# Attention, gated MLP and soft mixture of experts on one core: matmuls of constants, another order of loads and a moved subtraction in the opening

## The chip, the core and the metric

One core of a Trainium2 chip runs the whole program. It has a matrix engine (TensorE; PE in the profile, its weight loads PEld), three engines for elementwise work (VectorE or DVE, ScalarE or ACT, GpSimd or POOL), a queue engine that issues transfers (SyncE, SP), and 16 DMA engines. Each engine works through its own instructions in program order and waits on semaphores for the others.

The metric is the device time of one execution in microseconds (us). The kernel before takes 543.9 us, the median of three runs that lie between 542.54 and 544.36.

## The reference

Three stages follow one another; the change is in the first, attention with a forgetting gate.

```python
def _attn_ref(q, k, v, f):                      # q, k, v: (4, 8, 576, 64), f: (4, 8, 576)
    scores = scale * np.matmul(q, k.transpose(0, 1, 3, 2))
    cum = np.cumsum(np.log(np.clip(f, 0.0001, 1.0)), axis=-1)
    decay = cum[:, :, :, None] - cum[:, :, None, :]
    scores = np.where(causal, -1000000000.0, scores + decay)
    attn = np.exp(scores - np.max(scores, axis=-1, keepdims=True))
    attn = attn / (np.sum(attn, axis=-1, keepdims=True) + 1e-09)
    return np.matmul(attn, v)

x = attention, laid out as 2304 tokens x 512
h = x @ w_in;  x = (h * sigmoid(h)) @ w_out     # 512 -> 2048 -> 512
return soft_moe(x, phi, w1, w2)                 # 8 experts with 4 slots each, 512 -> 1024 -> 512
```

## The kernel before, in words

The 32 heads are worked off as 16 pairs. A pair's q and k come in one tile (`UB` for pair 0, `qk` after it) of 128 partitions x 2 heads x 576 positions: partitions 0 to 63 hold q, 64 to 127 hold k. The products run in a reduced-precision form of float32, so each operand is split into a high half (a rounded copy, `split_hi`, line 160, on ScalarE) and a low half (what the rounding lost, `split_lo`, lines 166 and 168, a subtraction). `QA` and `KA` hold the high halves of q and k, one over the other in partitions 0 to 63; in partitions 64 and up they hold what adds the decay: two rows of `KA` are the cumulated log gates of a head (`spread`, lines 174 and 176, small transfers), the rows of `QA` that meet them are ones, and row 127 of `QA` later takes the row maxima. `KB` and `QB` hold high and low halves crosswise, so that KA x QA plus KB x QB is the whole score.

Two passes are made over each head. `max_piece` (line 190, tile `mx`, six pieces m0 to m5 a head) multiplies KA with QA alone, and VectorE takes the row maxima (line 196, and 193). Three banks of PSUM turn over for these pieces. `max_fin` transposes the maxima (line 209, tile `mtp`), copies them (line 211) and sends them into row 127 of QA (line 212). `s_piece` (lines 236 and 238, tile `st`, pieces s0 to s4) makes the scores, and ScalarE writes their exponentials to `E` (line 242). GpSimd cuts the diagonal blocks (line 259). `av` (line 293) and `row_sums` (line 277) use E afterwards.

The order of all this is a string, `ORDER`, worked off once for each step i from -6 on, its first half for even i and its second for odd i. In step i the scores of head i and the maxima of head i+3 are made, so the first three heads have their maxima made in steps -3, -2 and -1, without scores beside them, and head 3 in step 0 beside the scores of head 0. The letters q0 to q3 in the first and second half are the four copies of `split_hi`: 0 is QA, 1 KA, 2 the high half in KB, 3 that in QB, in the order q2, q0, q1, q3; for pairs 0 and 1 they come in the steps -4 to -1, two steps a pair. z00 to z11 are the subtractions of `split_lo`. For pair 0 those for k are issued by the main loop itself after step -2, and go to VectorE; all other subtractions go to GpSimd.

Before step -6 `setup` prepares gates, masks and constants: VectorE fills, clips, scans and scales the gates into `cum`, ScalarE takes the logarithm, GpSimd fills the rest. Then the transfers are issued on SP: pair 0 (line 141, two transfers, one a head), the constant rows of QA for pair 1 (line 115, `init_q(1)`), the first head of pair 1, the decays of pairs 0 and 1 (four transfers), the second head of pair 1, the constant rows for pair 2, and pair 2 (line 138). The maxima of a pair need its QA and KA copies, its decays and its constant rows.

After attention come the MLP (`h`, lines 579 to 581) and the mixture of experts, whose code is the same in both kernels.

Of the kernel before, what the change touches and what calls it, by code (L numbers as in the profile page):

```python
# [9 lines left out]
F32 = mybir.dt.float32  # L10
F32R = mybir.dt.float32r
BF16 = mybir.dt.bfloat16
# [19 lines left out]
RING_A, RING_B, RING_T = "014", "235", "b"  # L32
# [3 lines left out]
def tile_attention_moe_softmoe(ctx: ExitStack, tc: tile.TileContext, qk, vr, f, wcat, phi, w1, w2, out):  # L36
# [44 lines left out]

    xs = [xpool.tile([128, 4, CH], F32, name=f"x{c}", tag=f"x{c}", bufs=1) for c in range(NCH)]

    def setup():
        nc.sync.dma_start(out=ft, in_=f)
        nc.vector.memset(c8, 1.0)
        init_k(0)
        init_q(0)
        nc.vector.tensor_scalar(ft, ft, 1e-4, 1.0, ALU.max, ALU.min)
        nc.scalar.activation(ft, ft, AF.Ln)  # L90
        nc.vector.memset(nbias, -float(896 << 23))
        nc.scalar.activation(warm, nbias[0:1], AF.Exp)
        nc.vector.tensor_tensor_scan(c8, c8, ft, 0.0, ALU.mult, ALU.add)
        nc.vector.tensor_scalar(cum[:, 0], c8, -8.0, None, ALU.mult)
        nc.vector.scalar_tensor_tensor(cum[:, 1], c8, -8.0, cum[:, 0], op0=ALU.mult, op1=ALU.subtract)
        nc.gpsimd.memset(mask, 0.0)
        nc.gpsimd.affine_select(out=mask[:, 320:448], in_=mask[:, 320:448], pattern=[[-1, 128]],
                                compare_op=ALU.is_ge, fill=-1e30, base=0, channel_multiplier=1)
        init_k(1)
        nc.gpsimd.memset(ones, 1.0)  # L100
        one = xs[8][:, 0, 0:128]
        nc.gpsimd.memset(one, 1.0)
        nc.gpsimd.affine_select(out=ident, in_=one, pattern=[[-1, 128]], compare_op=ALU.is_equal,
                                fill=0.0, base=0, channel_multiplier=1)
        init_k(2)
        for j in range(3):
            init_e(j)
# [25 lines left out]
    def load(p, hs=(0, 1)):  # L133
        b, hp = divmod(p, NP)
        if p not in staged:
            staged[p] = UB if p == 0 else ld.tile([128, 2, S], F32, name="qk", tag="qk", bufs=3)
        if p > 1:
            nc.sync.dma_start(out=staged[p], in_=qk[b, hp])
            return
        for h in hs:  # L140
            nc.sync.dma_start(out=staged[p][:, h], in_=qk[b, hp, :, h])
# [11 lines left out]
    def split_hi(p, j):  # L153
        q, k = staged[p][0:64], staged[p][64:128]
        qa = QA[p % 3][0:64, :, 64:640]
        if j == 3 and p > 1:
            nc.sync.dma_start(out=QB.of(p)[0:64].bitcast(F32), in_=qa.bitcast(F32))
        else:
            out = (qa, KA[p % 3][0:64], KB.of(p)[64:128], QB.of(p)[0:64])[j]
            nc.scalar.activation(out, (q, k, k, q)[j], AF.Copy)  # L160

    def split_lo(p, which, h):
        src = staged[p][:, h]
        eng = nc.vector if p == 0 and which == 1 else nc.gpsimd
        if which:
            eng.tensor_tensor(KB.of(p)[0:64, h], src[64:128], KB.of(p)[64:128, h], ALU.subtract)  # L166
        else:
            eng.tensor_tensor(QB.of(p)[64:128, h], src[0:64], QA[p % 3][0:64, h, 64:640], ALU.subtract)  # L168
# [12 lines left out]
    def max_piece(i, j):  # L181
        p, h = divmod(i, 2)
        qa, ka = QA[p % 3], KA[p % 3]
        blk = min(j, 4)
        k0, w = [(0, 64), (0, 192), (0, 320), (0, 448), (0, 288), (288, 288)][j]
        if j == 0 and h == 0:
            Mt[p] = att.tile([128, 2, 5], F32, name="Mt", tag="Mt", bufs=2)
            Mx[p] = att.tile([128, 2, 1], F32, name="Mx", tag="Mx", bufs=2)
        t = bank("b", [128, 512], "mx")
        nc.tensor.matmul(t[:, 0:w], lhsT=qa[0:127, h, 128 * blk:128 * blk + 128], rhs=ka[0:127, h, k0:k0 + w],  # L190
                         start=True, stop=True)
        if j == 4:
            nc.vector.tensor_reduce(Mx[p][:, h], t[:, 0:w], axis=AX.X, op=ALU.max)
        else:
            junk = att.tile([128, 448], BF16, name="junk", tag="junk", bufs=2)
            nc.vector.tensor_tensor_reduce(out=junk[:, 0:w], in0=t[:, 0:w], in1=mask[:, 448 - w:448], scale=1.0,  # L196
                                           scalar=Mx[p][:, h] if j == 5 else -3e38, op0=ALU.add, op1=ALU.max,
                                           accum_out=Mt[p][:, h, blk:blk + 1])
        if j == 5:
            MAXED.add(i)  # L200
# [134 lines left out]
    def att_step(i, cv):  # L335
        p, h = divmod(i, 2)
        s = 0 <= i < NH
        pa = p - 1
        a = 0 <= pa < NPAIR
        mi = i + 3  # L340
        mx = 0 <= mi < NH

        def cvt(n, ph):
            if ph == 0:
                conv_b(n)
            elif ph == 1:
                conv_c(n)
            elif ph == 2:
                conv_d(n, 0)
                conv_d(n, 1)  # L350
            elif ph == 3:
                conv_wh(n)
            elif ph == 4:
                conv_d(n, 2)
                conv_d(n, 3)
            elif ph == 6:
                conv_wl(n)
                conv_f(n)

        for op in ORDER.split("|")[h].split():  # L360
            k, j = op[0], op[1:]
            if k == "s" and s:
                s_piece(i, int(j))
            elif k == "m" and mx:
                max_piece(mi, int(j))
            elif k == "v" and a:
                av(pa, int(j))
            elif k == "r" and a and done["r"] <= pa:
                row_sums(done["r"])
                done["r"] += 1  # L370
            elif k == "q" and 0 <= p + 2 < NPAIR:
                split_hi(p + 2, int(j))
            elif k == "z" and j[0] == "1" and (i + 3) // 2 == 0:
                pass
            elif k == "z" and 0 <= (i + 3) // 2 < NPAIR:
                split_lo((i + 3) // 2, int(j[0]), int(j[1]))
            elif k == "f":
                max_fin()
            elif k == "n" and done["n"] < min(done["r"], NPAIR - 1):
                norm_b(done["n"])  # L380
                done["n"] += 1
            elif k == "b" and done["b"] < done["x"] and done["b"] in READY:
                norm_c(done["b"])
                done["b"] += 1
            elif k == "p" and 1 < p + 3 < NPAIR:
                spread(p + 3)
            elif k == "x" and done["x"] < done["n"]:
                norm_x(done["x"])
                done["x"] += 1
            elif k == "c":  # L390
                for n, ph in cv:
                    cvt(n, ph)
            elif k == "e" and p <= 0:
                max_fin()
            elif k == "k":
                cut()
            elif k == "g":
                pump()
            elif k == "w" and 0 <= p + 1 < NPAIR:
                load_v(p + 1)  # L400
            elif k == "l" and 3 <= p + 3 < NPAIR:
                load(p + 3)
# [562 lines left out]
    with tc.manual_schedule():  # L965
# [5 lines left out]
        for i in range(-6, NH + 2):  # L971
            if i == -6:
                load(0)
                init_q(1)
                load(1, (0,))
                spread(0)
                spread(1)
                load(1, (1,))
                init_q(2)
                load(2)  # L980
                nc.sync.dma_start(out=cumd, in_=cum.bitcast(F32))
            if i in (0, 3, 5):
                mo["cap"] += 1
            if i == 0:
                pump()
            if i == NH - 6:
                ld.release()
                mo["r"] = tc.alloc_tile_pool(name="w1p", bufs=1, side="right", reuse_waits="tile")
                FREE.extend((mo["r"], f"r{j}") for j in range(4))
            cv = [(n, i - b) for n, b in enumerate(CONV_AT) if 0 <= i - b < 7]  # L990
            att_step(i, cv)
            if i == -2:
                split_lo(0, 1, 0)
                split_lo(0, 1, 1)
            if i == NH + SEL:
                mo.update(last=LAST)
                pump()
            if i == NH - 1:
                selectors()
                split_x(0)  # L1000
            elif i == NH:
                FREE.append((nrm, "U2"))
                arena_a()
                split_x(1)
# [215 lines left out]
```

## Time and profile before

| | |
|---|---|
| median of three runs | 543.9 us |
| the profiled execution | 545.5 us, its span 543.8 us |
| PE busy | 506.0 us, 93% of the span |
| DVE, ACT, POOL busy | 335.3, 296.8 and 206.9 us |
| start of the first maxima, the first scores, the first `av` | 9.37, 20.58 and 34.83 us |

The span runs from the first to the last instruction; the execution's own time has 1.7 us around it. PE's 93% is a mean: in the first 40th of the span it is 2 tenths, in the second 6, and from the third (27 us) on mostly 9. [...] The column of the granted clock begins with a fixed 1.00 in this trace, so that in the opening the level is read from the spacing of equal matmuls.

### The profile page before, as it was taken

How to read it: one execution, taken by the hardware profiler on the slowest of the kernel's cores; microseconds unless marked ns; L12 is line 12 of the kernel's file. 1: busy time of each engine (PE TensorE's matmuls, PEld its weight loads, DVE VectorE, ACT ScalarE, POOL GpSimd, SP SyncE). 2: the span in 40 equal slices, each digit the busy share in tenths (PEclk: the TensorE clock that was granted, in tenths of full speed). 3: DMA queues.
4: the chain of work that ended last, by engine and by line, in shares of the span. 5: the costliest groups of instructions: out<-in, count | busy, mean ns of one | idle time of the engine just before them, and what ended most of it. 6: DMA issues, size and time to landing. Idle time of an engine off the chain costs nothing.

```text
span 543.8 us, 11207 instructions
## 1 busy us (share of the span) xinstructions
PE 506.0 (93%) x4115; PEld 374.2 (69%) x4115; DVE 335.3 (62%) x892; ACT 296.8 (55%) x585; POOL 206.9 (38%) x226
## 2 busy tenths in 40 slices
PE   2699999999999999899999999999997999999994
PEld 2487878877777777677776777666664676664562
DVE  6657767776889379998888733565653532335013
ACT  6668989898896666467556553323321433332013
POOL 6478788887888403556447400000000000001000
PEclk9999999999999999999999999999998999999998
DMA  5435575466654467402512109789697728677998
GB/s 147 157 94 172 164 223 170 133 193 165 174 160 103 130 234 298 176 39 65 170 36 121 78 2 317 224 212 296 211 321 216 242 92 328 230 292 274 409 384 330
DMA packets 43819, 105.80 MB, mean 195 GB/s; under 512 B 8148, under 2 KB 16628, under 8 KB 43764
## 3 DMA queue, kind: packets, MB, share of 16 engines
q1 hardware_dynamic: 43764, 105.08, 59.3%
q8 instruction: 32, 0.52, 0.4%
q14 instruction: 23, 0.19, 0.1%
HBM read 82.58 MB, written 17.52 MB: 184 GB/s over the span
## 4 chain that ended last, share of the span: by engine, by line
PE 68%; DVE 11%; DMA 8%; ACT 7%; issue 2%; POOL 2%; SPq 1%; DVEq 0%; POOLq 0%; ACTq 0%
PE h L579 9%; PE h L581 8%; PE h L580 8%; PE av L293 6%; PE mx L190 4%; PE st L236 4%; PE rs L277 4%; PE st L238 4%; DMA gr<-far 3%; PE lp L650 3%; PE gtp L623 3%; PE pp L766 3%; PE so L892 3%; PE h L837 3%; DVE wt L482 1%
## 5 line engine op out<-in xcount | busy, mean ns | idle before, releaser
L579 PE MATMUL h<-w,xh 128*128 128x512 f32 x288 | 119.3, 414 | 3.7 <-DVE gt L600 3.7
L581 PE MATMUL h<-w,xh 128*128 128x512 f32 x288 | 114.2, 397 | 0.0
L580 PE MATMUL h<-w,xl 128*128 128x512 f32 x288 | 114.1, 396 | 0.0
L600 DVE SCALAR_TENSOR_TENSOR gt<-gt,h 128x512 f32<-128x512 f32 (+1 forms) x73 | 48.4, 674 | 70.5 <-ACT gt L593 70.5
L593 ACT ACTIVATE gt<-h 128x512 f32<-128x512 f32 (+1 forms) x73 | 42.7, 590 | 86.4 <-PE h L581 76.5
L242 ACT ACTIVATE E<-st 128x256 f32<-128x256 f32 (+4 forms) x160 | 63.6, 431 | 18.2 <-PE st L238 15.1
L196 DVE CUSTOM_DVE_ANT_0 junk<-mx,mask 128x64 bf16<-128x64 f32 (+3 forms) x128 | 50.0, 415 | 36.9 <-PE mx L190 35.5
L579 PEld LDWEIGHTS h<-w,xh 128*128 128x128 f32 x288 | 54.4, 189 | 22.0 <-DVE gt L600 6.1
L812 POOL MEMSET SM<- 128x512 f32 x2 | 1.1, 531 | 177.8 <-ACT gt L593 175.2
L190 PE MATMUL mx<-KA,QA 127*128 127x64 f32 (+2 forms) x192 | 53.4, 352 | 15.0 <-ACT KA L160 11.6
L581 PEld LDWEIGHTS h<-w,xh 128*128 128x128 f32 x288 | 54.5, 189 | 12.9
L580 PEld LDWEIGHTS h<-w,xl 128*128 128x128 f32 x288 | 54.5, 189 | 11.0
L236 PE MATMUL st<-QA,KA 128*128 128x256 f32 (+2 forms) x192 | 57.6, 310 | 3.9 <-DMA QA<-mr 1.5
L259 POOL TENSOR_SCALAR_AFFINE_SELECT E<-E 128x256 f32<-128x256 f32 (+1 forms) x96 | 42.9, 461 | 31.4 <-ACT E L242 30.3
L238 PE MATMUL st<-QB,KB 128*128 128x256 f32 (+2 forms) x192 | 53.5, 303 | 0.0
L293 PE MATMUL av<-E,VF 128*64 128x320 f32 (+4 forms) x448 | 50.8, 364 | 0.0
L190 PEld LDWEIGHTS mx<-KA,QA 127*128 127x128 f32 x192 | 35.9, 209 | 20.6 <-issue 9.3
L166 POOL TENSOR_TENSOR KB<-qk,KB 64x576 fp32r<-64x576 f32 x30 | 42.4, 1433 | 4.1 <-ACT KB L160 3.1
L168 POOL TENSOR_TENSOR QB<-qk,QA 64x576 fp32r<-64x576 f32 x30 | 42.8, 1428 | 2.5
L236 PEld LDWEIGHTS st<-QA,KA 128*128 128x128 f32 x192 | 36.2, 188 | 8.2 <-ACT E L242 7.3
L293 PEld LDWEIGHTS av<-E,VF 128*64 128x64 f32 x448 | 29.5, 136 | 17.8 <-POOL E L259 0.3
L510 POOL TENSOR_TENSOR raw<-raw 128x512 f32<-128x512 f32 x16 | 25.4, 1590 | 38.8 <-ACT raw L499 31.8
(152 smaller groups left out, 830.7 us busy)
## 6 DMA issues: line engine op xcount, KB each, us to landing
unit<-in_w_dram SPq DMA_DIRECT2D x64, 512.0 KB
raw<-in_w_dram SPq DMA_DIRECT2D x32, 512.0 KB
far<-gb SPq DMA_DIRECT2D x16, 512.0 KB
gr<-far SPq DMA_DIRECT2D x64, 128.0 KB
qk<-in_qk_dram SPq DMA_DIRECT2D x14, 576.0 KB
VF<-in_v_dram SPq DMA_DIRECT2D x16, 320.0 KB
RB<-R SPq DMA_DIRECT2D x32, 144.0 KB
out_dram<-ob SPq DMA_DIRECT2D x18, 256.0 KB
```

Of the source, the lines that this page charges most:

```text
L168: eng.tensor_tensor(QB.of(p)[64:128, h], src[0:64], QA[p % 3][0:64, h, 64:640], ALU.subtract)
L190: nc.tensor.matmul(t[:, 0:w], lhsT=qa[0:127, h, 128 * blk:128 * blk + 128], rhs=ka[0:127, h, k0:k0 + w], start=True, stop=True)
L196: nc.vector.tensor_tensor_reduce(out=junk[:, 0:w], in0=t[:, 0:w], in1=mask[:, 448 - w:448], scale=1.0, scalar=Mx[p][:, h] if j == 5 else - ...
L236: nc.tensor.matmul(t[0:m, o:o + n], lhsT=ka[:, h, k0:k0 + m], rhs=qa[:, h, 64 + q0:64 + q1], start=True, stop=False)
L238: nc.tensor.matmul(t[0:m, o:o + n], lhsT=kb_[:, h, k0:k0 + m], rhs=qb[:, h, q0:q1], start=False, stop=True)
L242: nc.scalar.activation(e[0:m], t[0:m, 0:o], AF.Exp, scale=0.125)
L259: nc.gpsimd.affine_select(out=e, in_=e, pattern=pattern, compare_op=ALU.is_ge, fill=0.0, base=0, channel_multiplier=-1)
L293: nc.tensor.matmul(AVP[p][x][64 * h:64 * h + 64, o0:o0 + n], lhsT=VF[p % 2][:, kb, h], rhs=E[2 * p + h][kb][:, c:c + n], start=kb == 0, st ...
L579: nc.tensor.matmul(o, lhsT=xh[:, d, tok], rhs=w[:, 0], start=(d == 0), stop=False)
L580: nc.tensor.matmul(o, lhsT=xl[:, d, tok], rhs=w[:, 0], start=False, stop=False)
L581: nc.tensor.matmul(o, lhsT=xh[:, d, tok], rhs=w[:, 1], start=False, stop=(d == 3))
L600: nc.vector.scalar_tensor_tensor(g, g, 1.0, h[:, n * j:n * j + n], op0=ALU.add, op1=ALU.mult)
```

## The change

A new function `heat` issues matmuls on a constant tile (`hot`, 128x256 ones, written by VectorE first of all, in a tile that is used much later) into a bank of PSUM, and nothing reads what they leave there. 22 of 512 columns come at the start, one of 256 columns behind each piece of maxima in the steps before 0 (18 of them), and four of 256 columns at each `e` of these steps (three times, twelve in all, eight of them ahead of the first maxima). The loads of pair 1 are issued right behind those of pair 0, and the decays of pair 0 before the constant rows for pair 1. The copies of `split_hi` for pairs 0 and 1 run in the order QA, KA, KB, QB. The subtractions for k of pair 0 go to GpSimd.

```diff
+    hot = xs[7].rearrange("p a c -> p (a c)")[:, 0:256]
+
+    def heat(n, w=512):
+        t = ps.tile([128, 512], F32, name="st", tag="av" + RING_A[0] if RING_A[0] in "ab" else "b" + RING_A[0], bufs=1)
+        for _ in range(n):
+            nc.tensor.matmul(t[:, 0:w], lhsT=hot.bitcast(BF16)[:, 0:128], rhs=hot.bitcast(BF16)[:, 0:w],
+                             start=True, stop=True)
+
     def setup():
         nc.sync.dma_start(out=ft, in_=f)
+        nc.vector.memset(hot, 1.0)
+        heat(22)
         nc.vector.memset(c8, 1.0)
...
-        eng = nc.vector if p == 0 and which == 1 else nc.gpsimd
+        eng = nc.gpsimd
...
             elif k == "m" and mx:
                 max_piece(mi, int(j))
+                if i < 0:
+                    heat(1, 256)
...
-                split_hi(p + 2, int(j))
+                split_hi(p + 2, (1, 2, 0, 3)[int(j)] if p < 0 else int(j))
...
             elif k == "e" and p <= 0:
                 max_fin()
+                if i < 0:
+                    heat(4, 256)
...
             if i == -6:
                 load(0)
+                load(1)
+                spread(0)
                 init_q(1)
-                load(1, (0,))
-                spread(0)
                 spread(1)
-                load(1, (1,))
                 init_q(2)
                 load(2)
```

On SP, the opening before. `UB` is pair 0, `qk 128x576` a head of pair 1, `KA_87` and `KA_88` the decays of pairs 0 and 1, `QA_85` and `QA_86` the constant rows for pairs 1 and 2.

```order
L141 DMA UB<-in_qk_dram 128x576 x2
L115 DMA QA_85<-QA_84 64x1280
L141 DMA qk<-in_qk_dram 128x576
L174 DMA KA_87<-cum 2x1x576 x2
L174 DMA KA_88<-cum 2x1x576 x2
L141 DMA qk<-in_qk_dram 128x576
L115 DMA QA_86<-QA_84 64x1280
L138 DMA qk<-in_qk_dram 128x1152
```

And the same stretch of SP now.

```order
L151 DMA UB<-in_qk_dram 128x576 x2
L151 DMA qk<-in_qk_dram 128x576 x2
L184 DMA KA_87<-cum 2x1x576 x2
L125 DMA QA_85<-QA_84 64x1280
L184 DMA KA_88<-cum 2x1x576 x2
L125 DMA QA_86<-QA_84 64x1280
L148 DMA qk<-in_qk_dram 128x1152
```

Both heads of pair 1 now stand ahead of the decays, and the constant rows for pair 1 behind those of pair 0.

On VectorE, between the maxima of head 1 and those of head 2 before.

```order
L193 TENSOR_REDUCE Mx<-mx 128x1
L196 ISA junk,Mt<-mx,mask,Mx 128x288
L211 CAST mr<-mtp 5x128 x2
L166 TENSOR_TENSOR KB<-UB,KB 64x576 x2
L196 ISA junk,Mt<-mx,mask 128x64
```

And now.

```order
L203 TENSOR_REDUCE Mx<-mx 128x1
L206 ISA junk,Mt<-mx,mask,Mx 128x288
L221 CAST mr<-mtp 5x128 x2
L206 ISA junk,Mt<-mx,mask 128x64
L206 ISA junk,Mt<-mx,mask 128x192
```

The two subtractions are gone from VectorE; they stand on GpSimd behind those for q of pair 0 and ahead of those for k of pair 1.

On TensorE, the first maxima of head 0 before.

```order
L190 MATMUL mx<-KA_87,QA_84 128x64
L190 MATMUL mx<-KA_87,QA_84 128x192
L190 MATMUL mx<-KA_87,QA_84 128x320
L190 MATMUL mx<-KA_87,QA_84 128x448
L190 MATMUL mx<-KA_87,QA_84 128x288 x2
```

And now, from the last of the 30 matmuls that come ahead of them (`x_101` is the constant tile).

```order
L89 MATMUL st<-x_101 128x256
L200 MATMUL mx<-KA_87,QA_84 128x64
L89 LDWEIGHTS x_101
L89 MATMUL st<-x_101 128x256
L200 MATMUL mx<-KA_87,QA_84 128x192
L89 LDWEIGHTS x_101
L89 MATMUL st<-x_101 128x256
L200 MATMUL mx<-KA_87,QA_84 128x320
```

A matmul of constants stands behind each piece; from head 3 on the order of TensorE is as before.

## Rows read from the trace of the kernel before

**Rows 1.** Chain of waits up to 45 us: start us, us, what.

```profile
16.25 1.85 DVE KB L166 x2
...
26.29 1.17 ACT KA L160
```

**Rows 2.** Windows: us, busy of PE, PEld, DVE, ACT, POOL, PEclk, DMA, GB/s.

```profile
30.00:40.00 10.00, 10.00 (x104) 8.30 (x104) 4.92 (x19) 7.64 (x14) 6.64 (x10) 1.00 0.24 67
```

**Rows 3.** Timeline of PE up to 32 us: start us, us, what, [idle before <-releaser].

```profile
9.37 5.18 PE L190 MATMUL mx<-KA,QA 127*128 127x64 f32 x12 [9.37 <-ACT KA L160]
...
20.58 0.47 PE L236 MATMUL st<-QA,KA 128*128 128x256 f32 x1
...
21.60 0.57 PE L236 MATMUL st<-QA,KA 128*128 128x448 f32 x1
21.97 0.57 PE L238 MATMUL st<-QB,KB 128*128 128x448 f32 x1
...
25.49 0.30 PE L238 MATMUL st<-QB,KB 128*64 128x64 f32 x1
27.50 0.74 PE L190 MATMUL mx<-KA,QA 127*128 127x64 f32 x2 [1.71 <-ACT KA L160]
...
31.89 0.29 PE L238 MATMUL st<-QB,KB 128*64 128x64 f32 x1
```

**Rows 4.** Timeline of PE from 32 us on.

```profile
33.11 0.37 PE L236 MATMUL st<-QA,KA 128*128 128x448 f32 x1
33.31 0.36 PE L238 MATMUL st<-QB,KB 128*128 128x448 f32 x1
...
42.06 0.45 PE L190 MATMUL mx<-KA,QA 127*128 127x64 f32 x2
...
45.01 0.87 PE L293 MATMUL av<-E,VF 128*64 128x256 f32 x8
```

**Rows 5.** Timeline of ACT in the opening.

```profile
8.11 1.16 ACT L160 ACTIVATE KA<-UB 64x1152 fp32r<-64x1152 f32 x1
...
12.82 1.16 ACT L160 ACTIVATE KB<-qk 64x1152 fp32r<-64x1152 f32 x1 [2.37 <-DMA qk<-in_qk_dram]
...
15.18 1.16 ACT L160 ACTIVATE KA<-qk 64x1152 fp32r<-64x1152 f32 x1
...
21.30 0.97 ACT L242 ACTIVATE E<-st 128x256 f32<-128x256 f32 x2 [3.77 <-PE st L238]
22.59 0.54 ACT L242 ACTIVATE E<-st 128x448 f32<-128x448 f32 x1 [0.31 <-PE st L238]
```

**Rows 6.** Timeline of SP's queue in the opening.

```profile
6.87 2.58 SPq L174 DMA_DIRECT2D KA<-cum  x4
9.49 0.40 SPq L141 DMA_DIRECT2D qk<-in_qk_dram  x1
```

**Rows 7.** Timeline of DVE in the opening.

```profile
0.98 0.54 DVE L86 MEMSET fc<- 32x576 f32 x1 [0.98 <-PEq L1209]
...
15.95 0.28 DVE L211 CAST mr<-mtp 5x128 fp32r<-5x128 f32 x1 [0.28 <-PE mtp L209]
...
18.14 0.22 DVE L196 CUSTOM_DVE_ANT_0 junk<-mx,mask 128x64 bf16<-128x64 f32 x1
...
22.85 0.49 DVE L196 CUSTOM_DVE_ANT_0 junk<-mx,mask 128x320 bf16<-128x320 f32 x1 [1.06 <-PE mx L190]
```

**Rows 8.** Timeline of POOL in the opening.

```profile
8.17 2.77 POOL L168 TENSOR_TENSOR QB<-UB,QA 64x576 fp32r<-64x576 f32 x2 [0.58 <-ACT QA L160]
14.06 2.75 POOL L166 TENSOR_TENSOR KB<-qk,KB 64x576 fp32r<-64x576 f32 x2 [3.12 <-ACT KB L160]
```

**Rows 9.** Timeline of PE, behind the three longest waits after the opening.

```profile
214.53 0.50 PE L579 MATMUL h<-w,xh 128*128 128x512 f32 x1 [1.13 <-DVE gt L600]
...
229.39 0.50 PE L579 MATMUL h<-w,xh 128*128 128x512 f32 x1 [2.54 <-DVE gt L600]
...
413.79 1.16 PE L650 MATMUL lp<-gr,arena 128*32 128x256 f32 x16 [2.85 <-DMA gr<-far]
```

**Rows 10.** Windows of PE around these waits: us, busy, PEclk, DMA, GB/s.

```profile
212.00:216.00 4.00, 2.87 (x12) 1.00 0.77 245
228.00:232.00 4.00, 2.61 (x8) 0.79 0.01 2
412.00:416.00 4.00, 2.21 (x24) 0.83 0.27 105
```

## The prediction

> **What bounds the kernel now.** I read the page's parts first, then the windows, then the chain of waits up to 45 us, then the timelines of the engines in the opening. From 30 us on TensorE has no idle time at all, ten busy microseconds of ten, with ACT next at 7.64 [rows 2]; whatever brings the start of that stretch forward moves everything behind it, since nothing later in the program is tied to the clock on the wall, only to TensorE's progress and to transfers that are issued as pages come free. So the question is when that stretch begins and how fast its first microseconds run.
>
> Before it the chain goes through other engines. The first maxima begin at 9.37 [rows 3], just after ACT's copy into KA, 8.11 + 1.16 = 9.27 [rows 5]. Heads 0 and 1 are then paced by DVE to its second CAST, which ends at 15.95 + 0.28 = 16.23 [rows 7]. There the two subtractions for KB stand in the way, 1.85 us [rows 1], and the maxima of head 2 reach DVE only at 18.14 [rows 7]. Scores begin at 20.58 [rows 3], exponentials at 21.30 [rows 5]. ACT then alternates between these and the copies for pair 2, and its copy into KA, 26.29 + 1.17 = 27.46, releases the maxima of head 4 at 27.50 [rows 1, 3]. From there TensorE is the bound.
>
> The clock has to be read from equal matmuls. [...] Every matmul up to 32 us runs at the lower level. The rise, between the row at 31.89 and the one at 33.11, came after 4.8 us of unbroken work since 27.50; none followed the matmuls from 20.58 to 25.49, whose last ones had gaps between them.
>
> **The change, part by part.**
>
> *The 30 matmuls ahead of the first maxima.* VectorE's fill of 256 columns is 256/576 of the one that takes 0.54 us, 0.24, so TensorE starts at about 0.98 + 0.24 + 0.2 = 1.4 [rows 7]. 22 of 512 and 8 of 256 columns are 13,312 columns. [...] What else the first maxima need: KA, one ACT copy earlier, 9.27 - 1.16 = 8.11, plus 0.24 for the later start of the gates on VectorE; and the decays of pair 0, whose issue follows the gates too, at 6.87 + 0.24 = 7.1 [rows 6], and which in the kernel before took at most 9.37 - 6.87 = 2.5 us to be there, so 9.6 at the latest. First maxima at 9.0 to 9.6, against 9.37. I take +0.1 us, ends -0.4 and +3.0.
>
> [...]
>
> *Subtractions to GpSimd.* 1.85 us leave DVE's chain [rows 1]. What is late next is the copy of pair 1 into KA: it ended at 15.18 + 1.16 = 16.34 and waited 2.37 us for pair 1's second head [rows 5], issued only at 9.49 [rows 6]. With that load issued some 7 us earlier, and two copies where there were three, it ends at about 8.11 + 0.24 + 2 x 1.18 (KB and QB of pair 0) + 2 x 1.18 = 13.1, before DVE asks for it. Both edits are needed for the whole 1.85; the subtractions alone would give some 1.3. GpSimd takes 2.77 us for a pair of such subtractions [rows 8]; it is idle from 10.94 to 14.06, so those for pair 0 end near 13.7 and pair 1's near 17, against 16.81 before. The scores need pair 0's near 18.7: 5 us of cover. The two constant-row transfers, moved behind the decays of pair 0, are issued near 8.3 and 10; the maxima that need the first begin at about 16. Term: -1.85.
>
> *ACT in step 0.* From the first exponential to the end of the copy into KA, 21.30 to 27.46, ACT waits only 0.31 us that a row shows [rows 5]. A faster TensorE takes that away: -0.3, and no more, since the rest is ACT's own work.
>
> *The stage of head 1's scores and head 4's maxima.* [...] In this trace a wait of 2.54 and one of 2.85 us [rows 9] each let the clock fall, to mean levels of 0.79 and 0.83 in their windows, and one of 1.13 did not, 1.00 [rows 10]. So I let the clock fall once, just as head 4 begins, and come back some 3 to 5 us later as at 32 us before: term 0, ends -1.55 and +0.9 (lower level up to 2 us longer than the 4.5 of before, at half speed).
>
> [...]
>
> **Sum.** +0.1 - 0.2 - 1.85 - 0.3 + 0 = -2.25 us. The profiled execution took 545.5 us (span 543.8 and 1.7 around it), 1.6 above the median of the runs, so it would come to 543.25, and the median to 543.9 - 2.25 = 541.65, 541.6.
>
> **Rivals.**
>
> *The clock stays up through step 0.* Then the last stage gives its 1.55 too: -3.8, 540.1. [...] Against: the falls of [rows 9, 10].
>
> *The shift doesn't reach the end.* ACT has 7.64 us of 10 in the first full stretch [rows 2] and the pairs' loads come from the same queue; if step 2 waits for ACT or a load where it waited for TensorE before, most is given back there: about -0.5, 543.4. Against: before, TensorE alone had no gaps there, and the loads move forward with the steps that issue them.
>
> [...]
>
> **How the numbers follow.** Forecast 0.50, clock up 0.27, given back 0.15, constants the bound 0.08. 0.3% (1.6 us) is about what a measurement of this kernel tells from no change; the line is at 542.3. The forecast lies 0.65 us under it: I give it 0.8 faster and 0.2 the same; clock up is all faster, given back 0.1 faster and else the same, the last slower or the same in halves, with something over for slower causes not named. Faster 0.69, same 0.23, slower 0.08. The forecast's own range is 540.7 to 543.0, from its terms' near ends; with clock up and given back it is 539.6 to 543.8.
>
> **What would show it.** First maxima at 9.0 to 9.6, and equal constants that start twice as densely from some 5 or 6 us on. Head 2's maxima on DVE right behind the second CAST, near 16.2. ACT's first exponential near 19.2, its copy into KA for pair 2 done near 25.2. A drop in the granted clock near 25 us, or none: that decides between forecast and first rival. The first `av`, in the table of before at 34.83, near 32.6 or 31.1. It would be wrong if the first maxima came after 11, if the scores waited for GpSimd, or if the first `av` came 2 us earlier and the end did not.

## The result and the profile after

The changed kernel takes 539.43 us, the median of 20 runs between 537.32 and 542.11; beside them the kernel before took 544.65 on the same chip. The ratio is 0.990, with an interval from 0.9884 to 0.9915: faster by 1.0%, where 0.4% was forecast. Three later comparisons of the two unaltered kernels gave 0.9939, 0.9921 and 0.9929. By mean times the first gives a gain of 5.3 us and the three later ones together 3.8 (+/- 0.45, one standard error); all four put it at 4.4 (+/- 0.35), twice the 2.25 of the prediction. Ratios and mean differences leave out the few executions that lie more than 1.5% above the fastest of their kernel. The profiled execution took 540.85 us, its span 539.1.

The engines' busy time, from the page of the profile after.

```profile
PE 509.6 (95%) x4167; PEld 376.0 (70%) x4167; DVE 332.9 (62%) x891; ACT 296.0 (55%) x585; POOL 207.9 (39%) x228
```

PE is busy for longer than before (506.0 us) in a shorter span: the constants count as work, so that a share of busy time tells nothing of the gain. DVE's 335.3 us have become 332.9; the subtractions were 1.85 of them [rows 1].

TensorE, through the opening after (timeline: start us, us, what, idle before and what ended it; `...` stands for rows left out). `L89` are the constants, `L200` maxima, `L246` and `L248` scores.

```profile
1.25 8.55 PE L89 MATMUL st<-x 128*128 128x512 bf16 x30 [1.25 <-DVE x L94]
9.56 0.28 PE L200 MATMUL mx<-KA,QA 127*128 127x64 f32 x1
...
18.13 0.30 PE L246 MATMUL st<-QA,KA 128*128 128x256 f32 x1
...
18.69 0.36 PE L246 MATMUL st<-QA,KA 128*128 128x448 f32 x1
18.89 0.37 PE L248 MATMUL st<-QB,KB 128*128 128x448 f32 x1
...
21.58 0.27 PE L219 MATMUL mtp<-ident,Mt 128*10 128x128 f32 x1 [1.18 <-DVE Mt L206]
...
24.18 0.74 PE L200 MATMUL mx<-KA,QA 127*128 127x64 f32 x2 [2.23 <-ACT KA L170]
...
28.68 0.72 PE L200 MATMUL mx<-KA,QA 127*128 127x64 f32 x2
...
31.81 0.87 PE L303 MATMUL av<-E,VF 128*64 128x256 f32 x8
```

The first maxima stand where they stood, but the first scores begin at 18.13 instead of 20.58, head 4's maxima at 24.18 instead of 27.50 [rows 3], and the first `av` at 31.81 instead of 34.83. The two matmuls of 448 columns are 0.20 apart, where they were 0.37 apart [rows 3]: these scores run at the higher clock level, 0.45 ns a column where it was 0.83. The wait ahead of head 4 has grown from 1.71 to 2.23 us.

VectorE after, at the place where the subtractions stood.

```profile
15.69 0.28 DVE L221 CAST mr<-mtp 5x128 fp32r<-5x128 f32 x1 [0.18 <-PE mtp L219]
15.89 0.20 DVE L206 CUSTOM_DVE_ANT_0 junk<-mx,mask 128x64 bf16<-128x64 f32 x1
```

And ACT after, from pair 1's copy on.

```profile
11.47 1.16 ACT L170 ACTIVATE KA<-qk 64x1152 fp32r<-64x1152 f32 x1
...
18.59 1.25 ACT L252 ACTIVATE E<-st 128x256 f32<-128x256 f32 x3 [3.58 <-PE st L248]
19.86 1.16 ACT L170 ACTIVATE KB<-qk 64x1152 fp32r<-64x1152 f32 x1
...
22.97 1.16 ACT L170 ACTIVATE KA<-qk 64x1152 fp32r<-64x1152 f32 x1
```

Head 2's maxima follow the second CAST without a gap (18.14 before [rows 7]), and the first three exponentials stand in one unbroken row of 1.25 us, where they had a row of two, a wait of 0.31 and a third behind it [rows 5].

What the clock did, TensorE's windows after (window, its length, busy us and count, granted clock, DMA share, GB/s).

```profile
22.00:24.00 2.00, 0.00 (x0) 0.77 0.44 172
24.00:28.00 4.00, 3.82 (x14) 0.50 0.56 156
28.00:30.00 2.00, 2.00 (x12) 0.53 0.02 5
30.00:32.00 2.00, 2.00 (x16) 1.00 0.90 258
```

The level fell while TensorE waited ahead of head 4, stayed at 0.50 through that stage, and was back at 1.00 from about 30 us on.

### The profile page after: what moved, and what is told of

It is laid out like the page before. It is cut to its first block, busy times and chain, and to the rows that moved or that the text cites. A ratio compares the mean times of both kernels' runs of the same rounds, so it can differ in the third digit from the quotient of the medians.

```text
span 539.1 us, 11312 instructions
## 1 busy us (share of the span) xinstructions
PE 509.6 (95%) x4167; PEld 376.0 (70%) x4167; DVE 332.9 (62%) x891; ACT 296.0 (55%) x585; POOL 207.9 (39%) x228
## 4 chain that ended last, share of the span: by engine, by line
PE 64%; DMA 11%; DVE 11%; ACT 7%; issue 3%; SPq 2%; POOL 1%; DVEq 0%; ACTq 0%; POOLq 0%
PE h L593 8%; PE h L595 7%; PE h L594 7%; PE av L303 5%; PE mx L200 4%; PE st L246 4%; DMA gr<-far 4%; PE st L248 3%; PE rs L287 3%; PE gtp L637 3%; PE lp L664 3%; PE so L906 3%; PE h L851 3%; PE pp L780 2%; DMA unit<-WO 2%
## 5 line engine op out<-in xcount | busy, mean ns | idle before, releaser
L246 PE MATMUL st<-QA,KA 128*128 128x256 f32 (+2 forms) x192 | 56.8, 306 | 3.9 <-DMA QA<-mr 1.8
L200 PE MATMUL mx<-KA,QA 127*128 127x64 f32 (+2 forms) x192 | 51.0, 332 | 3.5 <-ACT KA L170 2.2
L248 PE MATMUL st<-QB,KB 128*128 128x256 f32 (+2 forms) x192 | 52.7, 299 | 0.0
L303 PEld LDWEIGHTS av<-E,VF 128*64 128x64 f32 x448 | 29.5, 136 | 17.8 <-POOL E L269 0.3
L246 PEld LDWEIGHTS st<-QA,KA 128*128 128x128 f32 x192 | 35.7, 186 | 8.1 <-ACT E L252 6.4
L200 PEld LDWEIGHTS mx<-KA,QA 127*128 127x128 f32 x192 | 33.8, 195 | 7.4 <-ACT KA L170 3.4
```

Of the source, the lines that this page charges most:

```text
L246: nc.tensor.matmul(t[0:m, o:o + n], lhsT=ka[:, h, k0:k0 + m], rhs=qa[:, h, 64 + q0:64 + q1], start=True, stop=False)
L248: nc.tensor.matmul(t[0:m, o:o + n], lhsT=kb_[:, h, k0:k0 + m], rhs=qb[:, h, q0:q1], start=False, stop=True)
L303: nc.tensor.matmul(AVP[p][x][64 * h:64 * h + 64, o0:o0 + n], lhsT=VF[p % 2][:, kb, h], rhs=E[2 * p + h][kb][:, c:c + n], start=kb == 0, st ...
```

## The experiments

Times are medians with the number of runs, each against runs of the kernel before on the same chip; a figure with +/- is a difference of mean times and its standard error. The openings quoted come from one profile a kernel.

### One part alone, or one undone

The change without its constants (run twice, with the same kernel):

```diff
-        nc.vector.memset(hot, 1.0)
-        heat(22)
...
-                if i < 0:
-                    heat(1, 256)
...
-                if i < 0:
-                    heat(4, 256)
```

> The change without any of its constant matmuls; loads, copies and subtraction as changed. [...] Rival (the constants carry the gain): first av later than 33.8, time within 1 us of before.

> The change without its constants, again. If the stretch from 329 to 452 us goes with the constants: 121.8 us or more there, as before; scatter: anything from 120 to 124. First av between 31.5 and 33, time 2 to 3 us below before.

Measured: 542.72 (12) against 544.77, ratio 0.9955 [0.9926, 0.9984], and 542.49 (11) against 544.75, 0.9951 [0.9925, 0.9977]; both together -2.4 us (+/- 0.4). TensorE of the first of them:

```profile
8.85 5.19 PE L198 MATMUL mx<-KA,QA 127*128 127x64 f32 x12 [8.85 <-DMA KA<-cum]
...
18.22 0.47 PE L244 MATMUL st<-QA,KA 128*128 128x256 f32 x1
...
25.14 0.47 PE L198 MATMUL mx<-KA,QA 127*128 127x64 f32 x2 [1.89 <-ACT KA L168]
...
28.70 0.72 PE L198 MATMUL mx<-KA,QA 127*128 127x64 f32 x2
...
31.72 0.87 PE L301 MATMUL av<-E,VF 128*64 128x256 f32 x8
```

Its maxima start 0.7 us sooner, since they wait for the decays alone. From there to head 4 it takes 16.29 us, and the changed kernel 14.62: 1.7 us are what the higher clock is worth up to head 4, and 0.96 of them remain as a lead there. But in this kernel the clock had risen by itself before head 4 (two score matmuls of 256 columns start 0.27 us apart at 18.22 and 0.14 apart at 25.44) and fell only when that stage had begun, as its windows show:

```profile
24.00:26.00 2.00, 0.86 (x6) 1.00 0.26 42
26.00:28.00 2.00, 2.00 (x10) 0.57 0.84 266
```

So its stage from 25.14 to 28.70 takes 3.56 us instead of 4.50, and at the first `av`, 31.72 against 31.81, the lead of the constants is gone. Over more profiles (two without constants, five of the changed kernel) it is 1.3 us at head 4 and 0.6 at the first `av` (31.77 and 31.21): half of it or more is lost in the stage that has no constants.

The constants alone, in the kernel before, with `hot` and `heat` as in the change (also twice):

```diff
+        nc.vector.memset(hot, 1.0)
+        heat(22)
...
+                if i < 0:
+                    heat(1, 256)
...
+                if i < 0:
+                    heat(4, 256)
```

> The kernel before with the constant matmuls alone; loads, copies and subtraction as before. Theory of the chain: first maxima near 9.6, VectorE still does the subtractions, head 2's maxima near 18, first av at 33.5 to 34.5, time 0.5 to 1.5 us below before. Rival (the constants carry the gain): first av near 32, time 3 to 5 us below before.

> The kernel before with the constants alone, again. If the stretch from 329 to 452 us goes with the constants: 121.7 us or less there; scatter: anything from 120 to 124. First av between 33 and 34.3, time 1 to 2 us below before.

Measured: 543.28 (12) against 544.77, ratio 0.9984 [0.9959, 1.001], and 542.75 (11) against 544.75, 0.9944 [0.9916, 0.9971]. The first is inconclusive by itself; together -1.6 us (+/- 0.45). The first `av` comes at 33.82 and 35.02, 0.6 us sooner in the mean than in five profiles of before (34.65 to 35.86, mean 35.01). So -1.6 alone and -2.4 without them add to -4.0, and the change's -4.4 needs no effect of the parts on each other. Only 0.6 of the 1.6 is seen in the opening, but its two profiles lie 1.2 us apart, so that this is not shown to be a difference. The order of the loads and that of the copies were not run by themselves.

The subtractions for k of pair 0 back on VectorE:

```diff
-        eng = nc.gpsimd
+        eng = nc.vector if p == 0 and which == 1 else nc.gpsimd
```

> The change with the two subtractions for k of pair 0 back on VectorE. Theory of the chain: 1.85 us come back between the second CAST and head 2's maxima, near 17.8; first av near 33.6; time 1.5 to 2 us above the change. Rival (the subtractions had cover): as the change, first av near 31.8.

Measured: 542.31 (12) against 544.77, ratio 0.9956 [0.9923, 0.999], mean difference -2.2 (+/- 0.7), which makes the moved subtractions worth 2.2 (+/- 0.8) of the change's 4.4. TensorE there, in head 2's maxima and at the first `av`:

```profile
18.28 0.47 PE L200 MATMUL mx<-KA,QA 127*128 127x448 f32 x1 [1.57 <-DVE Mt L206]
...
20.17 0.47 PE L246 MATMUL st<-QA,KA 128*128 128x256 f32 x1
...
27.06 0.74 PE L200 MATMUL mx<-KA,QA 127*128 127x64 f32 x2 [2.12 <-ACT KA L170]
...
33.84 0.87 PE L303 MATMUL av<-E,VF 128*64 128x256 f32 x8
```

With the loads and the constants in place, TensorE now waits 1.57 us for VectorE amid head 2's maxima, and what follows is late by 2.0 us at the scores, by 2.9 at head 4, as the clock had fallen at 20.0, and by 2.0 again at the first `av`, as it came back at 30.2 within head 4's stage, which took 3.89 us instead of 4.50. Against the mean of five profiles of the change the first `av` is late by 2.6. The 1.85 of the prediction was about right for the profile that it was read from. In five profiles of the kernel before, the two subtractions took 1.85, 2.19, 2.13, 2.50 and 2.65 us, always from 16.25 or 16.26 on. VectorE and, below it, GpSimd in the last of these:

```profile
16.26 2.65 DVE L166 TENSOR_TENSOR KB<-UB,KB 64x576 fp32r<-64x576 f32 x2
```

```profile
14.87 2.76 POOL L166 TENSOR_TENSOR KB<-qk,KB 64x576 fp32r<-64x576 f32 x2 [3.93 <-ACT KB L160]
```

In all eight profiles that have these two on VectorE they end 1.28 or 1.29 us after GpSimd's pair for k of pair 1, wherever they start (15.82 to 16.50); the second of them takes 0.74 or 0.75. From these ends I estimate that a part of their time goes with GpSimd's pair, which starts when pair 1's load and copy let it; no run tests this by itself.

### The clock held up through step 0

Constants of 256 columns where TensorE waits for head 3's maxima and for the copy into KA of pair 2 (run three times, with the same kernel):

```diff
+    def keep_up(n):
+        t = ps.tile([128, 256], F32, name="av", tag="ava", bufs=1)
+        for _ in range(n):
+            nc.tensor.matmul(t, lhsT=hot.bitcast(BF16)[:, 0:128], rhs=hot.bitcast(BF16)[:, 0:256],
+                             start=True, stop=True)
...
                 s_piece(i, int(j))
+                if i == 0 and j == "4":
+                    keep_up(16)
...
+                elif i == 0 and j == "5":
+                    keep_up(8)
```

> The change with 8 more constant matmuls of 256 columns behind head 3's last piece of maxima and 16 behind head 0's last scores, so that TensorE doesn't run dry before head 4. Theory of the chain: no drop of the granted clock near 23 us, the stage of head 1's scores takes 2.95 us in place of 4.5, first av near 30.2, 1.5 us earlier than with the change; time 1 to 2 us below the change. Rival (ACT is the bound of that stage): the clock stays up, first av within 0.5 us of 31.8.

> The change with constants in step 0 as well, again, beside the change on the same chip. If the 2.7 us by which its first av came earlier (29.1 against 31.8) reach the end: time 2 to 3 us below the change. If what follows gives them back: within 1 us of the change, and the rest from first av to the end 1.5 to 3 us longer than the change's.

> The change with constants in step 0 as well. First av near 29.3. Theory A: 5.4 us below before. Theory C: 3.5 to 4.5 below before.

Measured: 540.42 (10) against 544.77, ratio 0.9912 [0.9882, 0.9942]; 540.35 (9) against 543.75, 0.9925 [0.9893, 0.9958]; 539.46 (6) against 544.43, 0.990 [0.9876, 0.9924]. TensorE of the first:

```profile
21.35 1.92 PE L95 MATMUL av<-x 128*128 128x256 bf16 x16
23.75 0.47 PE L206 MATMUL mx<-KA,QA 127*128 127x64 f32 x2 [0.47 <-ACT KA L176]
...
26.21 0.45 PE L206 MATMUL mx<-KA,QA 127*128 127x64 f32 x2
...
29.11 0.87 PE L309 MATMUL av<-E,VF 128*64 128x256 f32 x8
```

And its windows.

```profile
24.00:28.00 4.00, 3.94 (x28) 1.00 0.67 171
28.00:30.00 2.00, 2.00 (x22) 1.00 0.74 267
```

This shows the mechanism of the first rival: with 0.47 us of idle time instead of 2.23 the clock doesn't fall (1.00 where it was 0.50), and the stage takes 2.46 us instead of 4.50; 2.95 were expected. The first `av` comes at 29.11, 29.58 and 29.82, 1.7 us sooner in the mean than in the changed kernel. The time doesn't show it clearly: -4.3 us (+/- 0.3) against the kernel before, as for the change itself; on the two chips where both were timed it was 0.84 and 0.93 us below the change by medians, with intervals that overlap. So neither a gain of 1.7 us on top of the change nor none at all is shown, and no version was found that beats the changed kernel clear of the noise.

### Does a shift of the opening reach the end?

The kernel just shown, with its first constants lengthened, `heat(22)` to 32 and to 42:

```diff
-        heat(22)
+        heat(32)
```

```diff
-        heat(22)
+        heat(42)
```

> As the run before this one, with 10 more constants of 512 columns at the start, which put the first maxima and all behind them 2.2 us later. First av near 31.5. Theory A: 2.2 us above that run. Theory C: less than 1.2 above it.

> The same with 20 more constants, 4.3 us later. First av near 33.6. Theory A: 4.3 us above the run without more, 1.1 below before. Theory C: less than 2.5 above it.

Measured: 542.04 (12), ratio 0.9963 [0.9935, 0.9991], and 545.75 (12), 1.0012 [0.9986, 1.0039], both against 544.43. TensorE in the longer one:

```profile
1.25 13.06 PE L89 MATMUL st<-x 128*128 128x512 bf16 x50 [1.25 <-DVE x L100]
...
34.04 0.87 PE L309 MATMUL av<-E,VF 128*64 128x256 f32 x8
```

Ten constants of 512 columns take 2.2 us at the higher clock (in the changed kernel's profile 11 of their loads fit into 2.30 us); the first `av` comes at 31.44 and 34.04, 1.9 and 4.5 us behind the mean of the kernel without them (29.50). The mean times lie 3.1 (+/- 0.8) and 5.8 (+/- 0.7) us above that kernel's on the same chip, and 2.4 and 5.0 above its three comparisons together. The first `av` at 34.04, 0.8 us sooner than in the table of before, goes with no gain at all. A later opening thus reaches the end about one to one or more; that it is swallowed behind the opening (the second rival) is refuted between 29.5 and 34 us. For the step from the change's 31.2 to 29.5 the times don't decide it.

### The unaltered kernels again

Nothing edited; the first three of these were timed, the last is one run with its profile, to see how the gain and the opening vary.

> The change, unaltered, timed beside the next run. Theory A (only the opening counts, one to one): first av between 31 and 32.5 again, time 3 to 4 us below before. Theory B (before's opening differs from execution to execution, since its clock rises late and at a different moment each time, and the constants take that away; the profiled execution of before was one of its better openings): time 4.5 to 6 below before, spread smaller than before's.

> The change a third time, beside three kernels that differ from one another in the length of the opening alone. First av near 31.4. Theory A (openings reach the end one to one, the rest is scatter): 2.1 us above the next run, 3.3 below before. Theory C (what follows gives part of an earlier opening back): within 1 us of the next run.

> The change again, timed. If the opening is all that the change moves: 3 to 3.6 us below before, first av near 31.5, and from first av to the end as long as before, 508 to 509 us in the mean of the profiles. If the rest belongs to it: 4.5 to 5.5 below, no fall of the clock near 410.

> The change, another profile. First av 30.9 to 32. If the missing fall near 410 belongs to the change: none. If it is scatter: about even odds.

The change: 541.19 (10) against 543.75, 0.9939 [0.9908, 0.9971]; 540.39 (8) against 544.43, 0.9921 [0.9893, 0.9949]; 540.46 (12) against 545.50, 0.9929 [0.9899, 0.9958]; one run of 539.56. First `av` at 30.92, 31.94, 29.95 and 31.44. The wait ahead of head 4 is 2.23 or 2.24 us in every one of these four profiles and in the first, and the clock falls within four of these waits; in the profile with the first `av` at 29.95 it fell only at 24.6, when that stage had begun, which then took 3.47 us instead of 4.50.

And the kernel before, one run with its profile each:

> The kernel before, unaltered, for a second profile of its opening. Theory B: first av elsewhere than at 34.83, most likely between 34 and 37, with the clock's first rise at another moment than 32.3. Theory A: first av within 0.5 us of 34.83.

> The kernel before, unaltered, a third profile. Theory B: again another first av and another moment of the first rise; the two move together. Theory A: first av within 0.5 us of 34.83.

> The kernel before, another profile. First av 34.6 to 34.9. If the fall near 410 belongs to before: a fall there again. If it is scatter: about even odds.

> The kernel before, another profile, with the same two expectations.

Times 543.8, 550.3, 548.06 and 544.49. Their openings don't vary enough to make the gain: the clock rose for the first time at 24.3 and 24.7 us in the first two, and in the profile that the prediction rests on only at about 32, yet the first `av` came at 34.65 and 34.69 against 34.83; the early rise was lost again at 27.7 and 28.1, at the end of the wait ahead of head 4 or just behind it, and head 4 itself began 0.3 us later, behind longer subtractions (2.19 and 2.13 us). What varies more is a late wait for a transfer. TensorE at it, in the second of these profiles, where it came twice:

```profile
413.21 1.41 PE L650 MATMUL lp<-gr,arena 128*32 128x256 f32 x16 [3.32 <-DMA gr<-far]
...
434.73 1.08 PE L650 MATMUL lp<-gr,arena 128*32 128x256 f32 x8 [3.79 <-DMA gr<-far]
```

The window around the second one, all engines (busy us of PE, PEld, DVE, ACT, POOL, then clock, DMA share, GB/s):

```profile
434.00:438.00 4.00, 3.27 (x24) 1.13 (x24) 0.00 (x0) 0.38 (x1) 0.00 (x0) 0.57 0.27 87
```

And the same wait in the changed kernel, with its window.

```profile
408.69 1.07 PE L664 MATMUL lp<-gr,arena 128*32 128x256 f32 x16 [1.84 <-DMA gr<-far]
```

```profile
406.00:418.00 12.00, 9.82 (x62) 1.00 0.77 198
```

In before the first of these waits was 2.85, 2.38, 3.32, 4.29 and 2.87 us in five profiles, and the clock fell behind all (0.83 to 0.86 in the mean of 406 to 418 us); in the change it was 1.84, 2.17, 3.03, 1.70 and 3.05, and it fell behind the two longest (0.86, and 1.00 in the other three). So the fall near 410 that the expectations ask for goes with the length of the wait in these ten profiles and not with the kernel alone.

## Why the prediction was right or wrong

The direction and the mechanism were right, the size was half of what came, and the time lies 0.2 us below the wider range (539.6 to 543.8). A part of that is the luck of the first comparison: the three later times of the changed kernel, 541.19, 540.39 and 540.46, lie inside it, with a gain of 3.8 us that is still more than forecast. The step that failed is the sum: its terms for what the clock shortens between the first maxima and head 4, -0.2 for heads 0 to 2 and "-0.3, and no more" for ACT, were too small (they came to -0.91 and -0.62), and the subtractions' -1.85 was read from the profile of before in which they were shortest. No run shows the terms +0.1 and -0.2 and the end of -1.55 as the prediction has them: the two first profiles gave +0.19 and -0.91, and 4.50 us for head 4's stage in both kernels, which took 2.46 with the clock held up. Point by point, each from the two first profiles:

- First maxima: 9.37 to 9.56, +0.19, for +0.1. Loads of the constants in TensorE's own rows show the rise at about 6.0, forecast for some 5 or 6 us:

```profile
5.06 0.15 PEld L89 LDWEIGHTS <-x 128*128 128x128 bf16 x1 [0.28 <-issue]
5.49 0.15 PEld L89 LDWEIGHTS <-x 128*128 128x128 bf16 x1 [0.28 <-issue]
5.92 2.30 PEld L89 LDWEIGHTS <-x 128*128 128x128 bf16 x11 [0.28 <-issue]
```

They start 0.43 us apart up to 5.92, and 11 of them fit into 2.30 us after it. That the constants are the bound, which had a chance of 0.08, is out, though they do hold up the first maxima, which start at 8.85 without them. The two longer versions show where they would decide: with the clock held up in step 0, 1.9 us (+/- 0.7) of gain were left with the first maxima at 11.45, and none with them at 14.07.
- Heads 0 and 1, from the first maxima to the end of the second CAST: 6.86 us before (9.37 to 16.23), 6.41 after (9.56 to 15.97), -0.45 for -0.2.
- Subtractions: from the end of that CAST to head 2's maxima 1.91 before and nothing after, -1.99 (the starts overlap by 0.08) for -1.85. Pair 1's copy into KA ended at 12.63, forecast at 13.1, and didn't stand in the way; GpSimd was done with pair 0's subtractions at 13.27, forecast near 13.7:

```profile
10.48 2.79 POOL L176 TENSOR_TENSOR KB<-UB,KB 64x576 fp32r<-64x576 f32 x2
```

- From head 2's maxima on VectorE to the first exponential: 3.16 us before (18.14 to 21.30), 2.70 after, -0.46. This stretch has no term of its own in the sum (the -0.2 was for heads 0 to 2 together); it holds head 2's last pieces and the two first score matmuls, which stand directly in the chain at the lower level (the first took 0.47 us there, and 0.30 after).
- ACT, from the first exponential to the end of the copy into KA: 21.30 to 27.46 before, 18.59 to 24.13 after, 6.16 to 5.54, -0.62 for -0.3. The reasoning "the rest is ACT's own work" took the one wait with a label, 0.31, for all there was. But the row ahead of it, 0.97 us for two exponentials [rows 5], had a gap of 0.15 inside, which a row of several instructions doesn't print, and exponentials that follow without a wait overlap a little: after, three take 1.25 together, where from 21.30 to the end of the third, at 22.59 + 0.54, it was 1.83. That is 0.58, nearly all of it.
- Head 4's stage: the wait was 1.71 us before and 2.23 after; the clock was forecast to fall once as the stage begins, and did, near 23. The stage takes 4.50 us in both kernels (27.50 to 32.00, 24.18 to 28.68): the term 0 holds. The next stage takes 3.13 instead of 2.83, +0.30, since the clock came back 1.2 us after its start (0.53 in the window up to 30 us, 1.00 from there).
- Together +0.19 - 0.45 - 1.99 - 0.46 - 0.62 + 0.30 = -3.03, which is the first `av`, 34.83 to 31.81. The forecast had 32.6.

The mean of five profiles of each kernel gives -3.8 for the opening (35.01 to 31.21); the terms above become -0.08, -0.50, -2.40, -0.47, -0.61 and +0.25. What is more than in the first pair lies ahead of head 4: the first maxima came at 8.93 to 9.66 in the change, as the clock rose at 4.2 to 6.2, and the subtractions took 2.27 us in the mean of before instead of 1.85.

That leaves 0.6 of the 4.4 behind the opening, with a standard error of about 0.55, so that nothing is shown there. The prediction's "whatever brings the start of that stretch forward moves everything behind it" was right, by the lengthened versions, though [rows 2] shows a TensorE without gaps only up to 40 us and [rows 9] has its waits behind. TensorE reaches the wait for `gr` at 405.7 us in the mean of the change and at 410.2 in before, 4.45 sooner, and waits there 2.4 instead of 3.1 us. But these profiled executions are 6.1 us apart in the mean, 1.7 more than the timings say, and from the first `av` to that wait TensorE took 373.3 to 376.2 us in before and 372.5 to 376.4 in the change, so that they can't place so small a rest. Whether the constants bring more than their opening shows (1.6 us against 0.6) was not settled either: the waits for `gr` of the two kernels with constants alone (2.13 and 2.74) and of the two without them (2.95 and 2.40), in the stretch that their second expectations speak of, don't tell them apart. In the kernel with the clock held up this wait was 3.06, 3.61 and 3.01, 0.9 us longer than in the change, so that about half of the 1.7 gained in its opening is waited away there, by these profiles; the cause of that is open.

## What to carry to other kernels

Where one engine runs without a gap from some point to the end, price the stretch ahead of it at the clock level that it will run at after the change, matmul by matmul along the chain and on the engines that it feeds, and take the gaps inside a row of several instructions from start and end, not from the printed wait. Matmuls that nobody reads held the clock here only as long as they went on: stopped ahead of a wait of 2.23 us, they lost half or more of their lead in the next stage (1.3 us to 0.6), where the clock was at 0.50. Where the same kernel varies by several us from run to run, an edit worth 2 us needs its comparison repeated, and so does the profile: the row that the largest term was read from varied by 0.8 us in five of them.

## What the runs showed of the hardware

- The granted clock's column shows no level ahead of its first recorded change: it reads 1.00 in the opening of before, while equal matmuls there start 0.37 us apart and later 0.20 [rows 3, 4].
- With the constants starting at 1.25 us the first rise came between 4.2 and 7.0 us, in kernels that issue the same matmuls; and with 2.23 or 2.24 us of waiting ahead of head 4 in five of five profiles, the fall came between 21.8 and 24.6, so that the stage after it took 4.50 us in four of them and 3.47 in one. One profile of an opening is good to about 1 us.
- Behind the wait for `gr` the clock stayed up after 1.70, 1.84 and 2.17 us and fell after 2.38 and more, in the ten profiles of the two kernels; but in the two lengthened versions it stayed up after 2.73 and 2.64, so that no length of the wait divides the two. In the opening it fell within or soon after waits of 1.89 to 2.24 us, with thin work around them, and in the three profiles with constants and VectorE's subtractions also at 19.3 to 20.7, 0.6 to 2.1 us after a wait of 0.95 or 1.57.
- Two subtractions on VectorE that start beside two on GpSimd (64x576 each) end 1.28 or 1.29 us after GpSimd's, in eight profiles of eight; they took 1.72 to 2.65 us.
